# Presetting key rows two elements at a time, projecting values between the stabiliser's steps, and values one tile ahead in the first unit of an attention kernel

## The chip, the cores and the metric

The kernel runs on one core of one Trainium2 chip. The metric is the device time of one execution in microseconds. A profile is one execution of its own, with the begin and end of every instruction. The experiments ran in three groups, each on another chip and each with the kernel before beside it; across groups compare the ratios to it, not the medians.

The engines are TensorE (in profiles PE, its weight loads PEld), VectorE (DVE), ScalarE (ACT), GpSimd (POOL) and SyncE (SP), which issues most transfers. PSUM is the memory in which the kernel has TensorE put its results; to evict a tile is to copy it out of there. The granted clock is the share of TensorE's full clock that the profile records (1.00 full, 0.50 half).

## The reference

```python
def _A_ref(x, wqkv, wo):                  # B, S, D = 1, 2048, 512; 32 heads of 16
    qkv = (x @ wqkv).reshape(B, S, 3, H, Dh).transpose(2, 0, 3, 1, 4)
    q, k, v = qkv[0], qkv[1], qkv[2]
    p = softmax(einsum("bhqd,bhkd->bhqk", q, k) * Dh ** -0.5)
    return einsum("bhqk,bhkd->bhqd", p, v).transpose(0, 2, 1, 3).reshape(B, S, D) @ wo
def _B_ref(x, w_gate, w_up, w_down):      # F = 1792
    return (silu(x @ w_gate) * (x @ w_up)) @ w_down
g = sigmoid((A_x * gate_w).sum(-1, keepdims=True))
out = g * _A_ref(A_x, ...) + (1 - g) * _B_ref(A_x, ...)
```

Everything is bf16. The cost is the softmax: 32 x 2048 x 2048 exponentials.

## The kernel before

The work is cut into 32 units (a block of 512 queries by a group of four heads), each of 16 slots (a tile of 128 keys). For a slot TensorE makes four banks of scores; ScalarE exponentiates two banks at a time (`s_t` to `e_t`, 128 x 1024), VectorE a few banks from unit 1 on; then TensorE multiplies the exponentials with the values (`o_ps`). Scores carry their own stabiliser: each head has an extra key row of ones, against which the query carries minus a bound of its largest score. For head group 0 that needs, before the first score, the largest |k| of every key row (`kpart`), a small matmul of it with |q| (`bp0`), and an addition to the query.

The start, in the order in which it is emitted (the order on each engine is fixed by the program):

```python
for g in range(1, G):                     # the other seven head groups' key rows
    nc.vector.memset(kaug[:, g, :], 1.0)  # 128 x 2048 bf16 each
# ... small constants
# keys (kp0, two PSUM tiles) and queries (qp0) of head group 0: 20 matmuls as the input lands
act(out=q0r, in_=qp0, func=Copy)
for i in range(2):
    vec.tensor_reduce(out=kpart0[:, i:i + 1], in_=kp0[i], op=max, apply_absolute_value=True)
    vec.tensor_copy(out=ones_h[i], in_=onescol)
    act(out=kaug[:, 0, i-th half], in_=kp0[i], func=Identity, bias=ones_h[i], scale=1.0)
    # i == 0: kneg1 and aq0 = |q0r| on VectorE
# kneg0 on VectorE; the two masked queries q0[0][:, v] on VectorE
for tt in range(4):                       # the first four value tiles
    if tt == 3:
        bp0 = matmul(kneg0, aq0); two VectorE additions of bp0 to q0[0]
    # value tile tt: four matmuls into one of two PSUM banks, then ScalarE evicts it into vaug
```

The remaining twelve value tiles are spread over unit 0 by a pacer, which emits pieces of side work (2 matmuls each) by their deadlines in slots; and an output forces its value tile if it is not out yet:

```python
for tt in range(4, KT):
    v_chain[tt] = pace.add(v_pieces(tt), 0, tt + 5)
# in pv(), just before an output matmul:
    if n < KT and n in v_chain:
        force(v_chain[n])                 # emits the matmuls and VectorE's eviction
# which output may go next:
def pv_ready(now):
    # ...
    if done < SLOTS and done // KT == closed:
        # ... its exponentials are done
# in the main loop, where the ring of EB = 15 exponential tiles is full:
    if pairs[0] - min(e_left.values(), default=pairs[0]) >= EB - 1:
        next_pv()
        continue
```

```python
def q0_pieces(qb):                        # pieces: projection q (deadline d - 6), bound bd (d - 4, after q)
    # end of q:  q0[qb] from PSUM on VectorE (x2);  aq = mt[:, 4:6, :];  aq = |q0[qb]|
    # bound:     two matmuls of kneg0 with aq;  two VectorE additions to q0[qb]
```

The emission order is planned from a model of the engines' times, so a change in one place may move instructions everywhere after it.

## Time and profile before

| | before |
|---|---|
| time, median of 3 | 925.75 us (925.74 to 927.09) |
| span of the profile | 923.9 us |
| ScalarE busy | 874.4 us |
| first exponential starts | 27.39 us |
| last exponential starts | 914.07 us |

The lines of the profile are in the prediction below. In a timeline each line has the start, the duration, the engine, the operation with its tiles, and in brackets how long the engine had been idle and what released it.

### The profile page before, as it was taken

The numbers are of one execution on the slowest core, as the hardware profiler recorded it, in microseconds if no ns is written. First come the engines' busy times: TensorE is split into PE (matmuls) and PEld (weight loads), VectorE is DVE, ScalarE is ACT, GpSimd is POOL, SyncE is SP. The second block draws the span as 40 slices with busy tenths as digits, with TensorE's granted clock in tenths as the row PEclk, the third lists the DMA queues.
The fourth block names the chain that finished last, engine by engine and source line by source line (L and its number), as shares of the span: only waits on it lengthen the run. The fifth ranks groups of instructions, "written<-read, shape, count | busy, mean of one in ns | idle before, by whom it ended". The sixth has DMA issues, their size and how long they took to land.

```text
span 923.9 us, 14142 instructions
## 1 busy us (share of the span) xinstructions
PE 819.3 (89%) x5073; PEld 219.1 (24%) x5168; DVE 744.2 (81%) x1032; ACT 874.4 (95%) x967; POOL 7.1 (1%) x29
## 2 busy tenths in 40 slices
PE   3979899999999888999998899899999989888985
PEld 1222222222222222222222222222222222222221
DVE  7349999899887879987778889877888798887784
ACT  2879999999999999999999999999999999999996
POOL 3000000000000000000000000000000000000000
PEclk9999999999999999999999999999999999999999
DMA  8300121131100112110001121110001111100000
GB/s 222 80 1 6 38 44 42 27 64 27 30 9 24 38 32 65 35 41 18 8 6 31 37 61 41 36 38 8 3 12 39 41 53 35 30 10 5 23 1 23
DMA packets 87534, 31.97 MB, mean 35 GB/s; under 512 B 75120, under 2 KB 87016, under 8 KB 87464
## 3 DMA queue, kind: packets, MB, share of 16 engines
q1 hardware_dynamic: 86408, 30.94, 13.6%
q8 instruction: 40, 0.66, 0.3%
q10 hardware_dynamic: 1056, 0.13, 0.1%
q14 instruction: 30, 0.25, 0.1%
HBM read 20.83 MB, written 2.34 MB: 25 GB/s over the span
## 4 chain that ended last, share of the span: by engine, by line
PE 40%; ACT 39%; issue 11%; DVE 9%; ACTq 0%; DMA 0%; DVEq 0%
ACT e_t L161 37%; PE s_t L158 16%; PE o_ps L158 9%; DVE y_t L167 4%; PE dps L158 3%; PE d_t L158 3%; PE gp L158 3%; PE up L158 2%; ACT th L161 2%; DVE kaug L228 1%; PE kp L158 1%; PE qp L158 1%; PE vp L158 1%; DVE u_t L167 1%; PE a_ps L158 1%
## 5 line engine op out<-in xcount | busy, mean ns | idle before, releaser
L161 ACT ACTIVATE e_t<-s_t 128x1024 bf16<-128x1024 f32 x902 | 848.5, 1043 | 19.6 <-PE s_t L158 15.0
L158 PE MATMUL s_t<-qx,kaug 64*128 64x512 bf16 x1692 | 353.8, 383 | 56.5 <-ACT e_t L161 50.4
L167 DVE TENSOR_SCALAR y_t<-d_t 128x512 uint16<-128x512 f32 x244 | 167.7, 687 | 76.3 <-PE d_t L158 74.4
L158 PE MATMUL o_ps<-e_t,vaug 128*32 128x512 bf16 x1804 | 192.9, 389 | 7.9 <-DVE vaug L167 4.6
L158 PEld LDWEIGHTS <-kaug 64*128 64x128 bf16 x2048 | 103.2, 93 | 345.4 <-issue 339.1
L167 DVE TENSOR_TENSOR u_t<-u_t,z_t 128x2048 f16<-128x2048 f16 x122 | 149.0, 1221 | 2.3
L158 PEld LDWEIGHTS <-vaug 128*32 128x32 bf16 x2048 | 53.9, 93 | 190.9 <-issue 181.6
L158 PE MATMUL d_t<-qx,kaug 64*128 64x512 bf16 x228 | 85.7, 376 | 0.0
L167 DVE TENSOR_TENSOR y_t<-y_t,u_t 128x2048 uint16<-128x2048 uint16 x61 | 74.4, 1220 | 0.8
L158 PE MATMUL dps<-wd_t,mt 128*128 128x512 bf16 x201 | 62.6, 384 | 3.0 <-issue 3.0
L158 PE MATMUL up<-xT,wu 128*128 128x512 bf16 x203 | 62.7, 384 | 2.4 <-issue 2.4
L158 PE MATMUL gp<-xT,wg 128*128 128x512 bf16 x198 | 62.0, 384 | 2.1 <-issue 2.1
L167 DVE SCALAR_TENSOR_TENSOR mt<-gs,up 128x512 bf16<-128x512 bf16 x56 | 38.2, 683 | 11.7 <-PE up L158 11.0
L167 DVE SCALAR_TENSOR_TENSOR gs<-th,gp 128x512 bf16<-128x512 bf16 x56 | 38.2, 682 | 8.3 <-ACT th L161 8.1
L167 DVE TENSOR_SCALAR u_t<-z_t 128x2048 f16<-128x2048 uint16 x61 | 42.2, 692 | 1.8
L167 DVE TENSOR_SCALAR z_t<-y_t 128x2048 uint16<-128x2048 uint16 x61 | 42.0, 688 | 0.8
L167 DVE TENSOR_SCALAR u_t<-u_t 128x2048 f16<-128x2048 f16 x61 | 41.9, 688 | 0.8
L167 DVE TENSOR_SCALAR y_t<-y_t 128x2048 uint16<-128x2048 uint16 x61 | 41.9, 687 | 0.6
L167 DVE CAST osb<-o_ps 128x512 bf16<-128x512 f32 x32 | 22.0, 688 | 19.7 <-PE o_ps L158 19.2
L161 ACT ACTIVATE th<-gp 128x512 bf16<-128x512 f32 x56 | 34.5, 616 | 0.0
L158 PE MATMUL o_ps<-y_t,vaug 128*32 128x512 bf16 x244 | 24.5, 389 | 5.8 <-DVE y_t L167 5.1
L158 PEld LDWEIGHTS <-mt 128*128 128x128 bf16 x263 | 16.2, 99 | 46.3 <-issue 39.7
(97 smaller groups left out, 317.4 us busy)
## 6 DMA issues: line engine op xcount, KB each, us to landing
wg<-in_B_w_gate_dram SPq DMA_DIRECT2D x56, 128.0 KB
wu<-in_B_w_up_dram SPq DMA_DIRECT2D x56, 128.0 KB
on<-osb SPq DMA_DIRECT2D x120, 16.0 KB
rb<-rr SPq DMA_DIRECT2D x15, 128.0 KB
wd_t<-in_B_w_down_dram SPq DMA_DIRECT2D x1, 1792.0 KB
qx<-qst SPq DMA_DIRECT2D x112, 16.0 KB
out_dram<-o_t SPq DMA_DIRECT2D x12, 128.0 KB
kaug<-on SPq DMA_DIRECT2D x20, 64.0 KB
```

The source lines that it names most:

```text
L158: ordered(nc.tensor.matmul(*args, **kw))
L161: ordered(nc.scalar.activation(*args, **kw))
L167: return lambda *a, **kw: ordered(f(*a, **kw))
L228: nc.vector.memset(kaug[:, g, :], 1.0)
```

## The change

The intent: get ScalarE, the fullest engine, to its first exponential sooner, and keep it fed in unit 0. Part 1 writes the constant rows as 4-byte elements whose two halves are both bf16 1.0. Part 2 projects the first value tiles between the stabiliser's steps and computes the bound before the fourth tile. Part 3 has the value tiles earlier and holds an output back until its tile is evicted.

```diff
-        nc.vector.memset(kaug[:, g, :], 1.0)
+        nc.vector.memset(kaug[:, g, :].bitcast(F32), 1.0019378662109375)
@@ the start
+    def v_now(tt):
+        for _, f, _ in v_pieces(tt, act_evac=True):
+            f()
     for i in range(2):
         vec.tensor_reduce(out=kpart0[:, i:i + 1], ...)
         vec.tensor_copy(out=ones_h[i][:], in_=onescol[:])
+        v_now(i)
         act(out=kaug[:, 0, ...], in_=kp0[i][:, :], ...)
     # kneg0
+    v_now(2)
+    bp0 = ps_d.tile([P, QBW], F32, tag="d", name="bp0")
+    mm(bp0[:, :], lhsT=kneg0, rhs=aq0[:, :], start=True, stop=True)
     # masked queries
+    # the two additions of bp0
-    for tt in range(V0):                 # (with bp0 and the additions at tt == 3)
-        for _, f, _ in v_pieces(tt, act_evac=True):
-            f()
+    v_now(3)
@@ unit 0
-        v_chain[tt] = pace.add(v_pieces(tt), 0, tt + 5)
+        v_chain[tt] = pace.add(v_pieces(tt), 0, tt + 3)
-        if done < SLOTS and done // KT == closed:
+        if done < SLOTS and done // KT == closed and not (now is not None and done in v_chain
+                                                          and not v_chain[done].done()):
         if pairs[0] - min(e_left.values(), default=pairs[0]) >= EB - 1:
+            for m in (done, done + 1):
+                while m in v_chain and not v_chain[m].out():
+                    emit_piece(v_chain[m])
             next_pv()
```

More of the change, by code (lines that the diff above doesn't have):

```diff
@@ L860 @@
                              op0=ALU.mult, op1=ALU.min)
+    v_now(2)
+    bp0 = ps_d.tile([P, QBW], F32, tag="d", name="bp0")
+    mm(bp0[:, :], lhsT=kneg0, rhs=aq0[:, :], start=True, stop=True)
     for v in range(2):
         vec.tensor_scalar(out=q0[0][:, v, :], in0=q0r[:, :], scalar1=vsel[:, v:v + 1], scalar2=None, op0=ALU.mult)
+    for v in range(2):
+        vec.scalar_tensor_tensor(out=q0[0][:, v, :], in0=bp0[:, :], scalar=vsel[:, v:v + 1],
+                                 in1=q0[0][:, v, :], op0=ALU.mult, op1=ALU.add)
     V0 = 4
-    for tt in range(V0):
-        if tt == V0 - 1:
-            bp0 = ps_d.tile([P, QBW], F32, tag="d", name="bp0")
-            mm(bp0[:, :], lhsT=kneg0, rhs=aq0[:, :], start=True, stop=True)
-            for v in range(2):
-                vec.scalar_tensor_tensor(out=q0[0][:, v, :], in0=bp0[:, :], scalar=vsel[:, v:v + 1],
-                                         in1=q0[0][:, v, :], op0=ALU.mult, op1=ALU.add)
-        for _, f, _ in v_pieces(tt, act_evac=True):
-            f()
+    v_now(3)
     plan.dve = plan.act = plan.pe
```

## The prediction

> **What bounds the kernel now.** I read the page first, for who is busy; then a table of busy time by stretches, for where that engine is not busy; then the timelines of those stretches. Busy time and the busy slices, from the page:
>
> ```profile
> PE 819.3 (89%) x5073; PEld 219.1 (24%) x5168; DVE 744.2 (81%) x1032; ACT 874.4 (95%) x967; POOL 7.1 (1%) x29
> ...
> ACT  2879999999999999999999999999999999999996
> ```
>
> ScalarE (ACT) works 874.4 of 923.9 us, nearly all of it on the 902 exponentials, 1.043 us each and about 0.93 us from start to start. The change removes no ACT work, so only the 49.5 us in which ACT is idle can shrink. The table of stretches (us busy on PE, PEld, DVE, ACT, POOL, then the granted PE clock, DMA share and GB/s) says where they are:
>
> ```profile
> 0.00:27.39 27.39, 12.76 (x42) 4.55 (x43) 19.27 (x40) 6.17 (x8) 7.05 (x29) 0.88 0.94 241
> 27.39:65.00 37.61, 31.39 (x189) 8.97 (x191) 13.91 (x21) 32.46 (x36) 0.00 (x0) 1.00 0.06 11
> 65.00:120.00 55.00, 50.95 (x324) 13.81 (x328) 50.31 (x72) 53.21 (x60) 0.00 (x0) 1.00 0.10 22
> 120.00:200.00 80.00, 77.01 (x512) 21.68 (x517) 73.11 (x105) 79.28 (x91) 0.00 (x0) 1.00 0.20 41
> ```
>
> ACT is idle 21.2 us before the first exponential (27.39 us), 5.2 us in unit 0 (27 to 65 us), then 1.8 and 0.7 us; the rest is 11.8 us over 700 us and 8.9 us at the end. The change works on the first two.
>
> The timeline of the start shows what holds the first exponential back (start, duration, engine, operation, in brackets the idle time before it and its releaser):
>
> ```profile
> 12.70 1.02 PE L158 MATMUL kp<-xT,mt 128*128 128x512 bf16 x4 [0.64 <-DMA xT<-in_A_x_dram]
> ...
> 14.47 1.89 PE L158 MATMUL vp<-rb,xT 128*128 128x512 bf16 x8 [0.54 <-DMA rb<-in_A_wqkv_dram]
> ...
> 14.62 1.76 DVE L228 MEMSET kaug<- 128x2048 bf16 x1 [0.38 <-issue]
> 16.76 1.76 DVE L228 MEMSET kaug<- 128x2048 bf16 x1 [0.38 <-issue]
> ...
> 18.45 1.21 DVE L167 TENSOR_REDUCE kpart<-kp 128x1 f32<-128x1024 f32 x1
> ...
> 22.48 1.08 ACT L161 ACTIVATE vaug<-vp 128x512 bf16<-128x512 f32 x2
> 23.12 1.86 PE L158 MATMUL vp<-rb,xT 128*128 128x512 bf16 x4 [6.76 <-ACT vaug L161]
> ```
>
> The first key projection is ready at about 13.3 us, but VectorE (DVE) presets the other key rows until 18.5 us, and only then takes the maximum (kpart) of which the stabiliser is made. ACT, in order, writes both key halves before it evicts any value tile (22.48), so TensorE stands still for 6.76 us; and value tile 2, the bound matmul and value tile 3 follow one another before the first score.
>
> In unit 0 the pattern near its end is this:
>
> ```profile
> 53.06 0.98 PE vp L158 x4
> 54.07 0.70 DVE vaug L167
> 54.81 0.40 PE o_ps L158 x4
> 55.22 0.54 PE s_t L158 x4
> ```
>
> These four are from the chain that ended last: a value tile is projected only when its output matmul is emitted; TensorE waits for VectorE's eviction of it, and the scores, and so the exponentials, queue behind.
>
> **What the Trainium skill says.** "VectorE: DVE Perf Modes", section "Zero memsets can be issued as uint32 (trn2)", says that a memset takes a cycle per element whatever the dtype. The trace agrees: 2048 bf16 elements take 1.765 us, 256 uint32 elements 0.272 us, 64 take 0.112 us, so 0.833 ns more per element both times; and the long presets start 2.14 us apart, 1.04 ns per element, the cycle of that page's 0.96 GHz. I use the start-to-start. "TensorE: Matmul & The Clock Gate", section "What's actually happening", has TensorE at half clock after an idle window of some 3.4 us. The trace agrees: after the 6.76 us of idleness the granted clock is 0.50 and the matmuls start 0.43 us apart, against 0.22 to 0.24 in the eight at 14.47. "PSUM — Partial Sum Buffer", "Specifications (TRN2)", gives 8 banks of 2 KiB per partition. The kernel's pools hold all eight (2 x 2 for score pairs, 1, 1, and 2 for all projections), so a third value tile cannot start before one of two is evicted; the wait at 23.12 is that.
>
> **Part 1, presets two at a time.** Removed: 7 memsets of 2048 elements, 2.14 us start to start. Added: 7 of 1024 4-byte elements, by the slope 0.112 + 960 x 0.000833 = 0.91 us long, some 1.09 us apart. VectorE saves 7 x 1.05 = 7.4 us and is done with them at about 18.5 - 7.4 = 11.1 us. Not all of it counts: the keys are ready only at 13.3 us, after the transposed input has landed (the 12.70 line). So the first maximum moves from 18.45 to about 13.4 us, 5.0 us, and then the DMA is the limit. The written bits are the same.
>
> **Part 2, value tiles between the steps.** No work is added: the same four tiles, in another order. With the durations of this trace (eviction 0.60 us, 0.5 apart; key copy 1.11, 1.0 apart; maximum 1.21): tile 0 matmuls 14.5 to 15.4, its eviction 15.5 to 16.1. VectorE: maximum 0 at 13.4 to 14.6, small steps to 15.3, maximum 1 to 16.5, kneg0 at 17.0, the two masked queries to 17.6. ACT: key half 0 at 16.0 to 17.1, tile 1 to 17.6, key half 1 to 18.7, tile 2 to 19.1, tile 3 to 19.6. TensorE: tile 1 to 16.4, tile 2 (bank free at 16.1) to 17.3, bound to 17.7, tile 3 behind it. VectorE adds the bound (1.41 us) from 17.8 to 19.2; the first score pair runs to 19.6. ACT and the scores are thus ready together, at about 19.7; with a few more semaphore delays 20.0. TensorE no longer idles long enough to go cold, which spares about 2 x 4 x 0.2 us that the old chain had. Gain at the first exponential: 27.4 - 20.0 = **7.4 us**, of which 5.0 is part 1 and 2.4 part 2.
>
> **Part 3, values one tile ahead.** The work is the same. Output matmuls of unit 0 now wait in the emission order until their value tile is evicted; deadlines are two slots earlier; and where the ring of 15 exponential tiles is full, two tiles are projected before the output. The waits of ACT on scores in this unit are 0.75, 1.45, 0.75, 0.96, 1.18 and (just after it) 0.35 us, 5.4 in all; TensorE's waits for an evicted value tile are 4.6 us in 6 times. TensorE has to fit 31.4 us of busy time into about 32.4 us of ACT time, 97%; it does 94 to 96% in 30 to 40 us with ACT fully busy, and may put off a few outputs (0.33 us each). I take **4.5 us** as gained, and 0.4 us as given back later, since outputs that lag fill the ring just when unit 1 must close.
>
> **Sum.** 7.4 + 4.5 - 0.4 = 11.5 us; the other 850 us have ACT about 98.5% busy, so an earlier start is passed on. 925.75 - 11.5 = 914.2, say **914.0 us**.
>
> **Rivals.** (a) The value weights take the place of the presets: tile 0 cannot start before the DMA that released it at 14.47, and ACT now evicts it before key half 0, so a later landing delays everything. For it: the queues are about full in this stretch (0.94). Against: VectorE's own steps reach 15.3 us anyway. It would cost 1 to 2 us: 915 to 916. (b) TensorE becomes the bound in unit 0 and the idleness of ACT merely changes its shape: part 3 gives 1 to 2 us and the kernel ends at 917. For it: 97%. Against: the six waits are empty time on both engines at once (PE 13.4 of 18.4 us in the second half of the unit). (c) The lag is paid back between units 1 and 2, where ACT already waits 0.9 us near 103 us: up to 2 us back. (d) The whole emission order is planned greedily from modelled times, so anything later may move either way, by 2 us I guess from the 11.8 us of scattered idleness.
>
> **Range and chances.** All rivals at once give about 919; no loss anywhere and luck with the later order about 910. Range 910.0 to 919.0. Faster by over 2% would need 18.5 us, more than the whole idleness of unit 0 and what the input DMA leaves of the start: 0.03. Slower by over 2%: 0.01. Within 2%: 0.96.
>
> **What would show it.** Presets 0.91 us each, done before 12 us; first maximum near 13.4 released by TensorE; first exponential near 20 us; no cold clock between 15 and 25 us; TensorE's waits for an evicted value tile under 1 us in unit 0 and ACT's there under 1.5; from then on both traces a constant 11 to 12 us apart. The prediction is wrong if the scheduler puts the presets between the stabiliser's steps, if the value weights land late, or if the gap between the traces shrinks after unit 0.

## The result, and the profile after

| | before | after | after, once more (control) |
|---|---|---|---|
| time, median | 925.91 us (4 runs) | 914.11 us (912.46 to 914.55, 4 runs) | 913.02 us (911.49 to 915.39, 4 runs) |
| ratio to before | | 0.9867 (0.985 to 0.9884) | 0.9859 (0.9841 to 0.9877) |
| span of the profile | 923.9 us | 912.8 us | 909.8 us |
| first exponential | 27.39 us | 21.31 us | 19.74 us |
| last exponential | 914.07 us | 901.71 us | 899.96 us |

A ratio is the mean time of one kernel's runs over that of the other's of the same rounds, so it is not quite the ratio of the medians; brackets are 95% intervals. Executions over 1.5% slower than the fastest of the same kernel are left out of the means. The kernel is 1.3 to 1.4% faster; results are correct.

The page of the kernel after, busy time and ScalarE's slices:

```profile
PE 819.2 (90%) x5074; PEld 218.2 (24%) x5168; DVE 737.7 (81%) x1032; ACT 873.2 (96%) x967; POOL 7.1 (1%) x29
...
ACT  3989999999999999999999999999999999999995
```

ScalarE's work is the same (873.2 us); its idleness is 39.6 us where it was 49.5. The table of stretches of the kernel after (busy us of PE, PEld, DVE, ACT, POOL, granted PE clock, DMA share, GB/s):

```profile
0.00:21.31 21.31, 12.08 (x39) 4.39 (x39) 13.52 (x40) 5.96 (x9) 7.08 (x29) 0.92 0.85 207
21.31:65.00 43.69, 40.12 (x237) 10.96 (x242) 21.25 (x34) 41.32 (x45) 0.00 (x0) 1.00 0.22 59
...
67.00:120.00 53.00, 50.77 (x322) 14.19 (x321) 48.72 (x69) 52.89 (x60) 0.00 (x0) 1.00 0.13 29
```

ScalarE is idle 15.4 us before the first exponential instead of 21.2, 2.4 us from there to 65 us, and 0.1 us in the 53 us to 120. The timeline of the start, after:

```profile
11.11 0.91 DVE L229 MEMSET kaug<- 128x1024 f32 x1 [0.16 <-issue]
...
12.20 1.02 PE L158 MATMUL kp<-xT,mt 128*128 128x512 bf16 x4 [0.97 <-DMA xT<-in_A_x_dram]
12.83 1.23 DVE L167 TENSOR_REDUCE kpart<-kp 128x1 f32<-128x1024 f32 x1 [0.78 <-PE kp L158]
...
15.26 4.44 PE L158 MATMUL vp<-rb,xT 128*128 128x512 bf16 x12 [1.82 <-DMA rb<-in_A_wqkv_dram]
...
17.13 0.60 ACT L161 ACTIVATE vaug<-vp 128x512 bf16<-128x512 f32 x1 [3.06 <-PE vp L158]
```

The presets end at 12.0 us and the first maximum now waits for the keys, as intended. But ScalarE waits 3.06 us for the first value tile, and that one for its weights (rb), which land at 15.26 us. Its four matmuls take until 17.1 us, 0.43 us each, since the clock is at half (the column before the last two, 0.53 and 0.50):

```profile
15.20:17.20 2.00, 1.94 (x5) 0.68 (x5) 1.47 (x5) 0.07 (x1) 0.00 (x0) 0.53 1.13 349
17.20:18.60 1.40, 1.40 (x5) 0.45 (x4) 0.00 (x0) 1.40 (x2) 0.00 (x0) 0.50 0.46 140
```

ScalarE's timeline through unit 0, after:

```profile
21.31 36.29 ACT L161 ACTIVATE e_t<-s_t 128x1024 bf16<-128x1024 f32 x38
57.76 5.61 ACT L161 ACTIVATE e_t<-s_t 128x1024 bf16<-128x1024 f32 x6 [0.17 <-PE s_t L158]
65.10 16.79 ACT L161 ACTIVATE e_t<-s_t 128x1024 bf16<-128x1024 f32 x18 [1.74 <-PE s_t L158]
```

All 32 exponentials of unit 0 and six of unit 1 follow one another without a wait. Six more follow after a wait of 0.17 us, and then there is one of 1.74 us that the kernel before does not have. TensorE's waits (from 19 to 120 us) name it:

```profile
PE bp L158 <- DVE mt L167: 1.7, 1, 1.7
PE s_t L158 <- ACT e_t L161: 1.5, 6, 0.3
PE o_ps L158 <- DVE vaug L167: 1.0, 3, 0.5
```

In the kernel before (27 to 120 us) the wait for evicted values was this:

```profile
PE o_ps L158 <- DVE vaug L167: 4.6, 6, 1.0
```

So TensorE's waits for evicted values are 1.0 us in all where they were 4.6, and the bound of a later query block waits 1.7 us for VectorE's absolute values.

To see where a difference arises I counted ScalarE's 902 exponentials in each trace and compared the start of the n-th with that of the kernel before (negative is earlier). The last column compares the ends of the spans. The profiled run is often not a typical one: it is the slowest of its kernel's runs for the kernel after, part 3 alone and the last four rows, and the fastest for the control and for parts 1 and 2 each alone:

| kernel (one profile each) | n = 0 | 40 | 44 | 100 | 250 | 901 | end |
|---|---|---|---|---|---|---|---|
| before, us from the start | 27.39 | 70.30 | 73.97 | 130.14 | 276.98 | 914.07 | 923.9 |
| after | -6.08 | -10.71 | -8.86 | -11.11 | -12.42 | -12.36 | -11.1 |
| after, control | -7.65 | -12.47 | -10.61 | -12.86 | -14.17 | -14.11 | -14.1 |
| part 1 alone | -7.16 | -6.93 | -6.93 | -6.92 | -6.93 | -6.90 | -6.9 |
| part 2 alone | -3.40 | -2.43 | -2.44 | -2.43 | -2.43 | -2.41 | -2.4 |
| parts 1 and 2 | -6.57 | -6.52 | -6.52 | -6.52 | -6.52 | -6.48 | -6.5 |
| part 3 alone | +0.73 | -4.12 | -2.26 | -3.02 | -4.32 | -2.93 | -1.6 |
| after, without the gate | -7.00 | -10.69 | -10.37 | -10.31 | -10.32 | -8.98 | -9.0 |
| after, old deadlines | -7.71 | -12.75 | -11.77 | -13.71 | -9.52 | -9.86 | -9.9 |
| after, bound before next queries | -6.63 | -11.44 | -11.34 | -13.33 | -12.41 | -11.76 | -10.7 |
| after, value weights from ScalarE's queue | -5.56 | -10.37 | -7.81 | -6.08 | -7.54 | -7.38 | -7.4 |

So the 11.1 us of the kernel after are: 6.1 at the first exponential, 4.6 won in unit 0, 1.85 given back in the one wait, 3.6 won by the 250th exponential, 1.3 lost at the very end.

### The profile page after: what moved, and what is told of

Same layout as the page of the kernel before. It is cut to its first block, busy times and chain, and to the rows that moved or that the text cites. A ratio compares the mean times of both kernels' runs of the same rounds, so it can differ in the third digit from the quotient of the medians.

```text
span 912.8 us, 14148 instructions
## 1 busy us (share of the span) xinstructions
PE 819.2 (90%) x5074; PEld 218.2 (24%) x5168; DVE 737.7 (81%) x1032; ACT 873.2 (96%) x967; POOL 7.1 (1%) x29
## 4 chain that ended last, share of the span: by engine, by line
PE 44%; ACT 38%; issue 11%; DVE 5%; SPq 1%; DMA 1%; ACTq 0%; DVEq 0%
ACT e_t L161 35%; PE s_t L158 18%; PE o_ps L158 9%; PE dps L158 3%; PE d_t L158 3%; PE gp L158 3%; DVE y_t L167 3%; PE up L158 2%; ACT th L161 2%; PE kp L158 1%; PE qp L158 1%; PE vp L158 1%; SPq L174 1%; DVE u_t L167 1%; DMA rb<-in_A_wqkv_dram 1%
```

## The experiments

My theory after the first look: the start and unit 0 add; at the start the value weights' landing has become the limit; the gain after unit 0 belongs to part 3; the 1.74 us wait and the late end are side effects. The rivals are with each run.

### Each part alone

**Part 1 alone.** The first hunk of the diff, nothing else.

> The kernel before with part 1 alone (the seven presets of other key rows as 4-byte elements). My theory (each part of the start helps, and they overlap): the presets end near 12 us, the first maximum starts near 12.8 us; the old order then still holds the second pair of value tiles behind the key copies, and the first exponential comes at 22 to 22.5 us instead of 27.39; the whole is 4.5 to 5.5 us shorter than before (about 921 us), unit 0 keeps its 5.4 us of waits. Rival A (parts 1 and 2 add up as predicted, 5.0 and 2.4 us): first exponential near 22.4, but then part 2 alone must give 2.4 us. Rival B (part 1 is nearly everything at the start, the order of the tiles little): first exponential at 21.3 to 21.6 and 6 us shorter.

Measured: 920.23 us, ratio 0.993 (0.9916 to 0.9943), 6.5 us. The first exponential is at 20.23 us, earlier than I or either rival expected. Its timeline (TensorE's third value tile, and ScalarE's first exponentials):

```profile
17.60 1.02 PE L158 MATMUL vp<-rb,xT 128*128 128x512 bf16 x4 [1.26 <-ACT vaug L161]
...
20.23 11.32 ACT L161 ACTIVATE e_t<-s_t 128x1024 bf16<-128x1024 f32 x12
```

Part 1 is worth 7.2 us here, not 5.0. The first maximum moved from 18.45 to 12.92, 5.5 us; and TensorE's wait before the third tile shrank from 6.76 to 1.26 us, so it no longer ran at half clock: from that tile to the first exponential it takes 2.63 us (20.23 - 17.60) against 4.27 (27.39 - 23.12), 1.6 us less. The two make 7.2. In unit 0 all waits remain (ScalarE 5.5 us).

**Part 2 alone.** The second hunk.

> The kernel before with part 2 alone (value tiles projected between the stabiliser's steps, the bound matmul before the last tile). My theory: the maximum still starts at 18.45 us behind the presets; tiles 0 and 1 no longer wait, but the bound matmul finds TensorE idle for several us and at half clock, so the first exponential comes at about 25 us, 2.4 us earlier than before; the whole is about 2.4 us shorter (923.5 us). If the gains of parts 1 and 2 add, this and the run with part 1 alone sum to more than the 6.1 us that both together gave; if less than 1 us, the order of the tiles counts for nothing without the short presets.

Measured: 924.31 us, ratio 0.9977 (0.9964 to 0.9989), 2.1 us. The first exponential is at 23.99; waits soon after it (the longest 0.63 us) leave 2.44 us, the expected 2.4. With part 1's 7.2 this would make 9.6; both together gave 6.1 to 7.7. The parts overlap. Here TensorE's wait only moves: the bound matmul waits 4.25 us for VectorE, and the clock is at half from 22.7 to 26.1 us.

**Part 3 alone.** The third hunk.

> The kernel before with part 3 alone (values one tile ahead of their outputs in unit 0). My theory: first exponential unchanged at 27.4 us; TensorE's 4.6 us of waits for evicted values fall under 1.5 us, and ScalarE's 5.4 us of waits in and just after unit 0 to about 2 us, one of them a new wait of some 1.7 us for the queries' absolute values of a later block; by then 3 us ahead of before, and a further 2 to 3 us are won in units 1 to 4, where the kernel before has scattered waits. Whole: 5 to 6 us shorter (920 us). Rival (later gain comes from the earlier start, not from part 3): only 2.5 to 3.5 us shorter.

Measured: 920.82 us, ratio 0.994 (0.9925 to 0.9956), 5.6 us. The profiled run (924.0 us) is the slowest of its six: the value weights landed late, at 15.95 us, and the clock fell twice, for a few us near 74 us (0.57) and near 306 us (0.58). Its own waits are as expected: ScalarE 0.2 us in unit 0, then the same 1.7 us of TensorE for VectorE's absolute values. From its own first exponential to the 40th it wins 4.85 us, and by the 250th 5.05.

**Parts 1 and 2, without part 3.** The third hunk taken out of the kernel after.

> The changed kernel without part 3 (parts 1 and 2 together). My theory: first exponential at 21.3 us as in the changed kernel, ScalarE's waits in unit 0 back to about 5 us, and the distance to the kernel before stays near 6 us to the end: 919.5 to 920 us, so part 3 is worth 5.5 us. Rival (the later gain comes from the earlier start): the distance grows to 8 to 9 us after unit 0, 917 us.

Measured: 918.88 us, ratio 0.9916 (0.9903 to 0.9929), 7.8 us. ScalarE's waits on scores between 20 and 70 us:

```profile
ACT e_t L161 <- PE s_t L158: 5.5, 6, 1.5
```

They are all back, and the distance to the kernel before stays at 6.5 us from the first exponential to the last (the table). So the rival falls: an earlier start by itself wins nothing later, and the 3.6 us after unit 0 come with part 3. From this kernel to the one after is 4.5 to 5.3 us by the ratios (0.9916 less 0.9867 or 0.9859). What part 2 adds to part 1 the times do not separate (0.9916 and 0.993, overlapping intervals).

### The pieces of part 3

The clause that emits two tiles ahead where the ring is full needs no run (a build in which it stops with an error passes): without it the program has the same instructions in the same order but for the numbers of tiles, so it never fires.

**Without the gate**, earlier deadlines kept.

```diff
-        if done < SLOTS and done // KT == closed and not (now is not None and done in v_chain
-                                                          and not v_chain[done].done()):
+        if done < SLOTS and done // KT == closed:
```

> The changed kernel without one piece of part 3: an output of unit 0 may again be emitted before its value tile is evicted; the earlier deadlines stay. My theory (the gate does the larger share of part 3, since without it an output still forces its tile and TensorE waits out the eviction): TensorE's waits for evicted values in unit 0 come to 2.5 to 4 us, ScalarE's there to 2.5 to 3.5 us, the queries' absolute values are computed in the old order, the 1.7 us wait is gone, and the whole is 1.5 to 3 us longer than the changed kernel. Rival (the earlier deadlines alone do it): waits as in the changed kernel, whole within 1 us of it or shorter.

Measured: 915.18 us, ratio 0.9874 (0.9857 to 0.9891). TensorE waits 1.5 us for evicted values (expected 2.5 to 4), ScalarE 1.6 us between 20 and 70 us, one wait of 1.03 us the largest; the 1.7 us wait is gone. From the first exponential to the 44th it gains 3.4 us, and then no more (a fall of the clock near 356 us, 0.66 from 356 to 360, costs it 1.3 us later): by then it has the 0.62 and 0.26 us waits near 93 us that the kernel before has near 103 us.

**Old deadlines**, gate kept.

```diff
-        v_chain[tt] = pace.add(v_pieces(tt), 0, tt + 3)
+        v_chain[tt] = pace.add(v_pieces(tt), 0, tt + 5)
```

> The changed kernel with the old deadlines of the value tiles, the gate kept. My theory: outputs lag further behind the exponentials, TensorE still waits little for evicted values (under 1.5 us), the ring of exponential tiles fills near the end of unit 0 and ScalarE waits there 1 to 2 us; whole 0 to 2 us longer than the changed kernel. Rival (the deadlines do it): ScalarE's waits in unit 0 return to 4 us or more and the whole is 4 us longer.

Measured: 914.36 us, ratio 0.9861 (0.9842 to 0.988). TensorE waits 1.2 us for evicted values, ScalarE 0.8 us once in and after unit 0. Its profile is 13.7 us ahead at the 100th exponential, more than any other in the table, and then loses 4.7 us at one place (by the 150th), where the clock is at half:

```profile
116.00:120.00 4.00, 2.88 (x17) 0.62 (x13) 3.43 (x5) 2.85 (x4) 0.00 (x0) 0.83 0.24 54
120.00:124.00 4.00, 4.00 (x21) 0.76 (x18) 2.70 (x4) 2.59 (x3) 0.00 (x0) 0.50 0.00 0
```

Either piece by itself does most of part 3; by the times the three cannot be told apart (0.9874, 0.9861, and 0.9867 or 0.9859). In the profiles the gate alone wins after unit 0 too (1.9 us from the 44th to the 100th, before its clock falls), the deadlines alone do not; that is one profile each.

### The new wait of 1.7 us

The timeline of the kernel after around it:

```profile
58.49 0.43 DVE L167 TENSOR_SCALAR mt<-on 128x1024 uint16<-128x1024 uint16 x1
...
61.97 1.40 DVE L167 TENSOR_SCALAR on<-qp,vsel 128x512 bf16<-128x512 f32 x2
...
63.40 0.43 DVE L167 TENSOR_SCALAR mt<-on 128x1024 uint16<-128x1024 uint16 x1
63.88 0.38 PE L158 MATMUL bp<-mt 128*128 128x512 bf16 x1 [1.70 <-DVE mt L167]
```

VectorE writes the absolute values of query block 2 (58.49), then, into the same buffer, those of block 3 (63.40), and only then does TensorE compute the bound of block 2. The program's order shows the same. In the kernel before, the bound comes between the two. So the change uncovered a missing dependence: block 2 of head group 0 gets block 3's bound, a wrong stabiliser. The result is still correct, since softmax does not depend on the stabiliser as long as nothing overflows.

The repair makes the next block's projection wait for the bound before it:

```diff
-    prev = []
+    prev, last_bd = [], []
...
-        q = pace.add(q, 0, d - 6)
+        q = pace.add(q, 0, d - 6, last_bd)
         bd = pace.add(bd, 0, d - 4, [q])
+        last_bd = [bd]
```

> The changed kernel with one dependence more: a later block's projection of head group 0 queries is not emitted before the bound matmul of the block before it. In the changed kernel the absolute values of block 3 overwrite those of block 2 before the bound of block 2 is computed, so TensorE waits 1.7 us for VectorE there, and the bound of block 2 is that of block 3 (harmless to softmax, which any stabiliser leaves the same). My theory: that wait falls under 0.6 us, ScalarE does not wait 1.7 us near 64 us, and the whole is 1 to 2 us shorter than the changed kernel. Rival (slack later in units 1 to 4 takes up the wait anyway): the gain is gone by the 250th exponential and the whole is within 0.5 us.

Measured: 913.21 us, ratio 0.9849 (0.9833 to 0.9864), the lowest, but its interval overlaps both of the kernel after. ScalarE's timeline has no such wait any more, only one of 0.17 us:

```profile
57.03 24.42 ACT L161 ACTIVATE e_t<-s_t 128x1024 bf16<-128x1024 f32 x26 [0.17 <-PE s_t L158]
```

At the 44th exponential this kernel has won 4.7 us since its first, where the kernel after has won 2.8; at the last one 5.1 us, where the kernel after has won 6.3. The three later profiles of kernels with this repair agree: 5.1 to 5.2 us at the last one. So the wait itself is removed as I expected, and the rival is right about its worth: what follows takes it up. From 59 to 265 us ScalarE waits 2.2 us here; from 65 to 265 us 0.5 us in the kernel after, its 1.74 us wait apart; from 70 to 277 us 3.1 us in the kernel before. ScalarE's waits on scores in these stretches, before and after (with the 1.74 us wait in it):

```profile
ACT e_t L161 <- PE s_t L158: 3.1, 10, 0.6
```

```profile
ACT e_t L161 <- PE s_t L158: 1.9, 2, 1.7
```

TensorE's own waits there point to VectorE. In the kernel before, outputs wait 1.4 us (four times) for VectorE's exponentials and 0.6 us for its copy of a finished unit's outputs, and the runs without part 3 and without the gate have the same; in the kernel after neither wait occurs; with the repair they are back, at 1.4 and 1.2 us.

### The landing of the value weights

In the profiles with parts 1 and 2, the first value tile's first matmul and the first exponential go together. In the six below that matmul waits for the weights:

| kernel | first value matmul | first exponential | difference | clock in between |
|---|---|---|---|---|
| after | 15.26 | 21.31 | 6.05 | half, then full |
| after, control | 14.76 | 19.74 | 4.98 | full |
| parts 1 and 2 | 15.85 | 20.82 | 4.97 | full |
| without the gate | 15.41 | 20.39 | 4.98 | full |
| old deadlines | 14.70 | 19.68 | 4.98 | full |
| bound before next queries | 15.78 | 20.76 | 4.98 | full |

**Value weights from ScalarE's queue** (they are behind four transposed loads on SyncE, whose issuing takes it until 9.78 us):

```diff
-    nc.sync.dma_start(out=wv, in_=A_wqkv[:, 2 * D:3 * D]...)
+    nc.scalar.dma_start(out=wv, in_=A_wqkv[:, 2 * D:3 * D]...)
```

> The changed kernel with the load of the value weights issued from ScalarE's queue instead of behind the four transposed loads of the input. My theory (the value weights have become what the first exponential waits for: 15.26 us landing plus 6.05): they land before 12 us, the first value tile follows the last query matmul at once, and the first exponential comes at 18.7 to 19.5 us, where the stabiliser's chain holds it; whole 1.5 to 2.5 us shorter than the changed kernel. Rival (the transfers share the same engines, so an earlier load of the weights delays the input by as much): the last key matmul moves from 12.2 to 13.5 us or later and the first exponential stays at 20.5 us or later.

Measured: 915.65 us, ratio 0.9874 (0.9851 to 0.9897), with runs from 912.49 to 918.23. The rival is right: the last keys came at 14.93 instead of 12.20 us, and the first exponential at 21.83 (in the slowest of the five runs, which was the one profiled). TensorE's timeline:

```profile
10.13 1.87 PE L158 MATMUL kp<-xT,mt 128*128 128x512 bf16 x4 [2.11 <-DMA xT<-in_A_x_dram]
...
14.93 1.86 PE L158 MATMUL kp<-xT,mt 128*128 128x512 bf16 x4
```

The four transposed loads hold SyncE for 11.8 us here, where they hold it for 8.9 in the kernel after and 9.5 in its control: as if the transfers shared what there is, sending the weights first only makes the input late. Here no transfer is waited for before the first value matmul (16.85), and the first exponential is again 4.98 us after it. From the first maximum (16.03) it is 5.80 us; in the six profiles of the table it is 6.4 to 8.5 us. So there, by these numbers, the stabiliser's steps had an estimated 0.6 us or more to spare, and the weights were what came last.

This profile also shows what the 1.7 us wait may cost. It has the same wait (TensorE's 1.70 us for the absolute values, ended at 64.22), but here TensorE's clock falls, and ScalarE waits 5.7 us in eight pieces between 58 and 80 us, of which the kernel after has 1.9 us (0.17 and 1.74) without a fall:

```profile
62.00:66.00 4.00, 2.30 (x12) 0.43 (x10) 3.01 (x6) 1.71 (x2) 0.00 (x0) 0.80 0.00 0
66.00:70.00 4.00, 4.00 (x19) 0.63 (x19) 2.37 (x3) 2.86 (x3) 0.00 (x0) 0.50 0.00 0
70.00:74.00 4.00, 4.00 (x16) 0.62 (x15) 1.02 (x2) 2.25 (x3) 0.00 (x0) 0.50 0.00 0
```

### The clock at the start and at the end

The kernel after ends 11.1 us after its last exponential starts, the one before 9.8 us. The first closing matmuls, before and after:

```profile
915.52 0.60 PE L158 MATMUL al<-wo_l,osb 128*128 128x512 bf16 x2
```

```profile
903.37 1.03 PE L158 MATMUL al<-wo_l,osb 128*128 128x512 bf16 x2
```

They take 1.03 instead of 0.60 us, at half clock. Of the first ten profiles three had this (after, part 3 alone, bound before next queries).

The next four runs went together. **The control:** the kernel after, unaltered.

> The changed kernel once more, unaltered, as a control on the chip of the next three. Expected: 913 to 914.5 us, first exponential at the landing of the value weights plus 5.0 us where TensorE's clock is full in the first value tiles, plus about 6 us where it is halved; the end 9.8 or 11.1 us after the last exponential starts, again by the clock.

Measured: 913.02 us, 0.9859 (0.9841 to 0.9877). The profile has full clock at both ends: first exponential 4.98 us after the first value matmul, end 9.8 us after the last exponential started, 909.8 us in all. Between the first and the last exponential it gains the same as the first profile of this kernel: 6.46 and 6.28 us.

**Eight idle matmuls before the value weights land** (with the repair):

```diff
+    keep = ps_d.tile([P, QBW], F32, tag="d", name="keep")
+    for _ in range(8):
+        mm(keep[:, :], lhsT=wpad[0][:, 0, :], rhs=xT[:, 0, 0:QBW], start=True, stop=True)
```

> The kernel with the added dependence (bound of a block before the next block's queries), and eight idle matmuls on TensorE between the last query matmul and the landing of the value weights, their result unread. Theory (in the changed kernel's profile the four first value tiles ran at half clock, which cost 1.05 us against the other runs): the first tiles run at full clock, the first exponential comes 5.0 us after the weights land (20 to 21 us), whole 0 to 1 us shorter than with the dependence alone, less spread. Rival (the clock there is a matter of the window's phase that these few matmuls do not settle): half clock there or no change in the times.

Measured: 914.37 us, 0.9865 (0.985 to 0.988). Full clock at the start (15.28, 20.27), but most profiles without these matmuls have that too, and the time is no shorter. Inconclusive on the clock, and no gain. The idle matmuls have a cost of their own, which I had overlooked:

```profile
13.56 1.89 PE L158 MATMUL keep<-xT,mt 128*128 128x512 bf16 x8
...
15.28 2.75 PE L158 MATMUL vp<-rb,xT 128*128 128x512 bf16 x12
```

They run right up to the first value matmul, while the semaphore of the weights' transfer is complete at 14.70 us: the value tile starts 0.58 us later than it could. So this run does not tell what a warm clock alone is worth. Here the closing matmuls were at half clock (1.04 us).

**Eight idle matmuls in the waits of the last few exponentials** (with the repair):

```diff
+        if len(pq) < 5:                    # after each of the last five score pairs
+            keep_busy(1)
+            keep_busy(1 if done < SLOTS - 1 else 2)     # before each of the last outputs
             emit_pv()
```

> The kernel with the added dependence, and eight idle matmuls in TensorE's waits for the last few exponentials, their result unread. Theory (three of ten profiles have half clock in the closing matmuls and an end 1.25 us later): full clock there, the end 9.9 us after the last exponential starts, whole 0.5 to 1 us shorter than with the dependence alone (912.2 to 912.7 us). Rival (they delay the last outputs by as much as they save, or do not hold the clock): no change or 0.5 us longer.

Measured: 913.41 us, 0.9855 (0.984 to 0.987), runs from 913.04 to 913.95. TensorE's timeline at the end:

```profile
902.32 0.60 PE L158 MATMUL keep_t<-xT 128*128 128x512 bf16 x2
...
903.23 0.60 PE L158 MATMUL al<-wo_l,osb 128*128 128x512 bf16 x2
```

Full clock, and an end 9.8 us after the last exponential. The ratio is not below that of the kernel without them (0.9849).

**Both.**

> The added dependence with both sets of idle matmuls. Theory: the two gains add, 911.5 to 912.5 us, the fastest of all and the least spread. Rival (the spread comes from when the value weights land, which none of this touches): 912.5 to 913.5 us with the spread as before.

Measured: 913.97 us, 0.986 (0.9845 to 0.9875), runs from 913.52 to 914.13. Full clock at both ends. Again the first idle matmuls outlast the landing (15.44) by 0.58 us, and the median is 0.56 us above that with the closing ones alone. The two kernels with the closing idle matmuls have the narrowest runs, 0.9 and 0.6 us wide, where the control is 3.9 wide; four runs each are too few to call that shown. No version beats the kernel after beyond its intervals.

## Why the prediction was right or wrong, point by point

- **The total** is right: 914.0 against 914.11 and 913.02 us. Its terms are not all right, and that it came so near is partly luck: the start gave 6.1 us in the first profile instead of 7.4 and the end lost 1.3, while what follows unit 0 won 1.7 net where 0.4 was to be given back.
- **The presets** are right: 0.91 us each (0.91 predicted), 1.07 us apart (1.09), done at 12.0 us (11.1; a copy after the first preset waits for its load until 5.35 us, which shorter presets do not move), the first maximum at 12.83 us released by TensorE (13.4).
- **The worth of parts 1 and 2 is the step that failed.** The text split 7.4 us into 5.0 and 2.4 and added them. Alone they are 7.2 and 2.4 us; together 6.1, 6.6 and 7.65 us in three profiles. The spared half clock, which the text put with part 2, is won by part 1 already: it follows from TensorE's shorter wait. And part 2 meets another limit.
- **Rival (a) came true.** The value weights set the first exponential: their landing plus 5.0 us in the five profiles of the table with full clock, and in that with the closing idle matmuls (15.25 and 20.23). They land at 14.7 to 15.9 us; the prediction used 14.47. For the same landing as in the run of part 1 alone (14.46) this gives 19.4 us, 0.8 us better than part 1's 20.23: an estimate of what part 2 adds, from those two numbers. It depends on the landing: in part 1 alone ScalarE takes up the first value tile only at 16.96 us, so there a landing at 15.3 would have cost nothing, and with part 2 it means 20.3, no earlier than 20.23 (an estimate too). Part 2 made the start hang on the weights.
- **"No cold clock between 15 and 25 us"** is wrong for the first profile: half clock from 15.3 to 18.6 us, 1.07 us (6.05 less 4.98). In the others it holds. Rival (a)'s cost of "1 to 2 us" was thus met by this profile, in part by the clock.
- **Unit 0** is right: 4.5 us predicted; 4.6 and 4.8 us from the first to the 40th exponential. TensorE's waits for evicted values are 1.0 us ("under 1 us"). The run without part 3 brings all 5.5 us of waits back and part 3 alone removes all but 0.2 us, so the cause is shown. Of the three pieces one never acts, and each of the other two suffices for most.
- **The give-back** was mis-sized and put on the wrong cause: 0.4 us for a full ring at the close of unit 1; instead 1.85 us, a wait for VectorE's absolute values emitted in another order. Rival (c), a loss between units 1 and 2, did not come.
- **"A constant 11 to 12 us from then on"** is wrong in its course: 8.9 us after unit 0, growing to 12.4. The 3.6 us won later were not predicted. They are in part the 1.85 us made good: net it is 1.7 us from the 40th to the 250th exponential, and the four repaired kernels, which lose next to nothing there, win 1.0 us in the same stretch. 2.6 us of them are waits of ScalarE that the kernel before has (3.1 us in ten waits from 70 to 277 us) and the kernel after does not (0.5 us besides its one long wait). They come with part 3, as the run without it shows, and of its pieces rather with the gate. TensorE no longer waits for VectorE's exponentials there; why the new order has them in time, and what the remaining 1.0 us are, stays open. Net, it is within the 2 us that rival (d) allowed, in the good direction.
- **The end** was not thought of: 1.3 us longer at half clock in the first profile, nothing in the control.
- Rival (b), TensorE as the bound in unit 0, fell: 38 exponentials follow without a wait.

## What to carry to other kernels

Two changes that shorten the same starting chain need not add: work out the second on the chain that the first leaves, and look which transfer it then meets. If an emission order is planned, a buffer shared by two chains of work needs a dependence between them, not an order that happened to hold; correct results did not reveal this one. Differences of under half a per cent are best read from counted steps in several profiles, since one fall of the clock can hide or make them.

## What the Trainium skill lacked or had wrong

- "TensorE: Matmul & The Clock Gate", section "Why this matters for your kernels", asks for no idle gap over some 3 us to keep the clock up. In these runs the clock fell with shorter ones: after a wait of 1.70 us in a stretch of 4 us with 2.3 us of work (so in two profiles with this wait, not in two others), and at the end of the kernel with waits of 0.5 us. So one gap of that length is not needed. Idleness that adds up over a stretch would fit: in each of the thirteen falls of these profiles (those of the last 5 us apart) TensorE was busy for at most 2.3 of the 3.4 us before. But in the kernel after it was busy for 2.2 of 4 us from 62 to 66 and the clock stayed, so no rule is shown. (Elsewhere the page speaks of short idle times between groups of matmuls that make the clock swing, without a length.)
- The same page, section "What's actually happening", has the full clock back after a busy window of some 3.4 us. At the start of the kernel after that fits (half clock for 3.3 us). In the run with the value weights first, TensorE was busy 4.00 of 4 us in both stretches from 66 to 74 us, as the profile models it, and the clock stayed at 0.50. ScalarE waited 5.7 us around that fall, 3.8 us more than without it: 0.4% of the span.
- "VectorE: DVE Perf Modes", section "Zero memsets can be issued as uint32 (trn2)", speaks of zero alone. A constant of two equal bf16 halves goes the same way: 2048 bf16 ones as 1024 4-byte elements took 0.91 us instead of 1.765, and 1.07 instead of 2.14 us from start to start.
- I found no page with how long a transposed load of this size holds the queue that issues it on this chip: four of 128 x 2048 held SyncE for 8.9 us, so the load behind them was issued at 9.78 us; with the value weights loading at the same time they held it for 11.8.
